# Opening of a fused attention and FFN kernel: v projected ahead of the scores, copies by one engine, more PSUM tiles, and the last output tile in two halves

## The chip, the core and the metric

One core of a Trainium2 chip. The metric is the time of one execution in microseconds (us), the median of several runs. A trace gives the span, from the first to the last instruction, which is some 1.8 us shorter than that time. All runs told here are of the fast state (granted TensorE clock 0.996 to 1.000 as a mean over the span). Within it, some executions, of either kernel, have a mean clock of 0.996 or 0.997; they take 0.5 to 2.3 us, mostly 1.5 to 2, longer than the other executions of the same kernel beside them (a clock halved for 3.4 us would be 0.997 over 520 us, and 1.7 us: an estimate from the run with late weights below). The ratios include them. Where it matters I also give the median of the executions with a clock of 0.998 or more, a cut that was made after the results were seen.

## The reference

Attention with keys and values projected along the sequence (from 1024 rows to 64), then a feed-forward layer with the quick Gelu on the joined heads:

```python
k_proj = np.einsum('ks,bhsd->bhkd', E, k)          # E, F: 64 x 1024; batch 8, heads 8, seq 1024, head dim 64
v_proj = np.einsum('ks,bhsd->bhkd', F, v)
scores = scale * np.matmul(q, k_proj.transpose(0, 1, 3, 2))
attn = softmax(scores)                             # cut: max, exp, sum
out = np.matmul(attn, v_proj)
x = out.transpose(0, 2, 1, 3).reshape(8192, 512)
h = x @ w_in                                       # 512 x 2048
g = h * (1.0 / (1.0 + np.exp(-1.702 * h)))
return g @ w_out                                   # 2048 x 512
```

## The kernel before

The FFN runs in 16 blocks of 512 tokens. In a block, 16 groups ("slots" 0 to 15) of four 128x512 matmuls make the hidden layer (FFN1), and 64 matmuls make the output (FFN2, eight more slots of eight). The attention of later blocks is put in between, at the slots named by `at(block, slot, ...)`. The order of every engine is fixed by the program. The program's PSUM tiles come from three pools: four general tiles (`ps_f`), two for token products (`ps_d`) and two for transposes (`ps_n`); a tile that comes round again must wait until its last reader is done.

The opening, before block 0 can start: heads are handled in pairs, `tok` multiplies exp(scores) with v and divides, `x_tr` transposes the result into `xT`, which FFN1 reads.

```python
    def v_out(b, v_ps, p0, n):                      # copies projected v out of PSUM
        for i in range(n):
            p = p0 + i
            for r, t in ((LO, p % 2), (HI, 1 - p % 2)):
                if b < 2:
                    cp = nc.scalar.copy if b == 0 and t == p % 2 else nc.vector.tensor_copy
                    cp(vxs[b][r, 2 * p + t, :D], v_ps[HI, 2 * i + t, :])
        # ... (the branch for b > 0)

    # tok(h, p, half): d_ps = ps_d.tile(...); 2 matmuls; rd = 1 / d_ps[..., D:]; x_sb = d_ps[..., :D] * rd   (VectorE)
    # x_tr(h, p, half): n_ps = ps_n.tile(...); 2 transposes; nc.vector.tensor_copy(xT ..., n_ps)

    # in ffn1, after the four matmuls into h_ps:
        if j > 0 or ts.start > 0 or fc > 4:
            nc.scalar.activation(gts[j][:, fc, ts], h_ps, AF.Gelu_apprx_sigmoid)
        else:                                       # tanh lives in the table of exp: no table switch yet
            t_sb = work.tile([P, n], F32, name="t_sb", bufs=3)
            nc.scalar.activation(t_sb, h_ps, AF.Tanh, scale=0.851)
            nc.vector.tensor_scalar(t_sb, t_sb, 0.5, 0.5, op0=ALU.mult, op1=ALU.add)
            nc.vector.tensor_tensor(gts[j][:, fc, ts], t_sb, h_ps, op=ALU.mult)

    # the opening, in TensorE's order
    for g in range(2):
        k_half(proj0(0, 4 * g, 4), g)               # k of heads 0-3, 4-7
        warm(3)                                     # fillers: matmuls on zeros
    q_tr(0, 0)()
    warm(3)
    for u in range(2):
        scores(0, u, 0)()
    v_out(0, proj0(1, 0, 4), 0, 2)                  # v of heads 0-3
    warm(2)
    tok(0, 0, 0)()
    tok(0, 1, 0)()
    # ... v of heads 4-5, x_tr, tok, v of heads 6-7, x_tr, tok, q_tr(0, 1), x_tr

    order = [(half, fc) for fcs in (range(12), range(12, FC)) for half in range(2) for fc in fcs]   # block 0
    at(0, 4, gelu_table)                            # switch ScalarE's table after slot 4
    # ... block 2:
        at(2, O + u, scores(4, u))
        at(2, O + 3 + u, scores(5, u))
    at(2, O + 5, norm(4, 0))
```

Block 0 is done in halves of 256 tokens: first slots 0 to 11 of the first half, so it can start with the attention of half the tokens. The order of the loads: E and F, k (two pieces), q (first quarter), v (three pieces), q (second quarter), input weights `w_in` in slices 0 to 5 of 256 columns, q (second half), slices 6 and 7, then `w_out`. Slice i serves slots 2i and 2i+1. They are issued by GpSimd, and every one waits until the load eight places ahead of it has landed.

```python
    for i in range(6):
        load_w_in(i)
    load_kv(q, qt, 0, "q0_sb", H, JB, JB)
    for i in range(6, 8):
        load_w_in(i)
```

The softmax here doesn't subtract the row's maximum and nothing guards it: scores larger than these inputs give would overflow.

Of the kernel before, what the change touches and what calls it, by code (L numbers as in the profile page):

```python
# [9 lines left out]
F32 = mybir.dt.float32  # L10
BF16 = mybir.dt.bfloat16
AF = mybir.ActivationFunctionType
ALU = mybir.AluOpType
# [4 lines left out]
def kernel(ctx, tc, q, k, v, E, F,  # L18
                                                     moe_w_in, moe_w_out, out):
    nc = tc.nc  # L20
    B, H, S, D = q.shape
    KP, _ = E.shape
    DM, DFF = moe_w_in.shape
    P = 128
# [92 lines left out]
    def f_tile(shape, dt=F32):  # L117
        return ps_f.tile(shape, dt, name="f_ps")

    def warm(n):  # L120
        w_ps = f_tile([P, TB])
        for _ in range(n):
            nc.tensor.matmul(w_ps, zeros[:, :P], zeros, start=True, stop=True)  # L123
# [25 lines left out]
    def proj0(e, h0, n):  # L149
        ps = f_tile([P, n, D])  # L150
        for j in range(J):
            nc.tensor.matmul(ps, eft[:, j, :], (kt, vt)[e][0][:, h0:h0 + n, j, :],  # L152
                             start=(j == 0), stop=(j == J - 1))
        return ps
# [11 lines left out]
                                ident[:KP, :KP])  # L166
        nc.vector.tensor_copy(kts[b % 2][:, p0:p0 + n, :], t_ps)

    def v_out(b, v_ps, p0, n):
        for i in range(n):  # L170
            p = p0 + i
            for r, t in ((LO, p % 2), (HI, 1 - p % 2)):
                if b < 2:
                    cp = nc.scalar.copy if b == 0 and t == p % 2 else nc.vector.tensor_copy
                    cp(vxs[b][r, 2 * p + t, :D], v_ps[HI, 2 * i + t, :])
        if b > 0:
            vv = v_ps[HI].rearrange("k (u x) d -> k u x d", x=4)
            for r, xs_ in ((LO, X_LO), (HI, X_HI)):
                nc.vector.tensor_copy(vqs[b % 2][r].rearrange("k (u e) d -> k u e d", e=2), vv[:, :, xs_, :])
# [44 lines left out]
    def scores(h, u, half=None):  # L224
        b, c = divmod(h, NB2)
        j0, n = (c * JB, JB) if half is None else (c * JB + half * JB // 2, JB // 2)
        ts = slice(j0 * P - c * TB, (j0 + n) * P - c * TB)

        def go():
            if h not in expT:  # L230
                expT[h] = att.tile([P, HP, TB], BF16, name="expT", bufs=3)
            s_ps = [f_tile([P, n * P]) for _ in range(2)]
            four(s_ps, [kts[b % 2][:, 2 * u + i, :] for i in range(2)],
                 [qT[b][:, j0:j0 + n, 2 * u + i, :] for i in range(2)])
            for i in range(2):
                nc.scalar.activation(expT[h][:, 2 * u + i, ts], s_ps[i], AF.Exp, scale=scale)  # L236
        return go
# [4 lines left out]
    def x_of(h):  # L242
        if h not in xT:
            xT[h] = att.tile([P, KC, TB], BF16, name="xT", bufs=3)
        return xT[h]
# [17 lines left out]

    def tok(h, p, half):
        def go():
            d_ps = ps_d.tile([P, 4, D + 1], F32, name="d_ps")
            for i in range(2):
                t = 2 * half + i
                nc.tensor.matmul(d_ps[:, 2 * i:2 * i + 2, :].rearrange("s t d -> s (t d)"),  # L269
                                 expT[h][:, p, t * P:(t + 1) * P],  # L270
                                 vxs[h // NB2][:, 2 * p:2 * p + 2].rearrange("r t d -> r (t d)"),
                                 start=True, stop=True)
            rd = work.tile([P, 4, 1], F32, name="rd")
            nc.vector.reciprocal(rd, d_ps[:, :, D:])  # L274
            xs[h, p, half] = work.tile([P, 4, D], BF16, name="x_sb", bufs=4)
            nc.vector.tensor_tensor(xs[h, p, half], d_ps[:, :, :D], rd.to_broadcast([P, 4, D]), op=ALU.mult)  # L276
        return go

    def x_tr(h, p, half):
        def go():  # L280
            x_sb = xs.pop((h, p, half)).rearrange("s (i t) d -> s i (t d)", i=2)
            n_ps = ps_n.tile([P, 2, P], BF16, name="n_ps")
            for i in range(2):
                nc.tensor.transpose(n_ps[:, i, :], x_sb[:, i, :], ident)  # L284
            nc.vector.tensor_copy(x_of(h)[:, p, half * TB // 2:(half + 1) * TB // 2],
                                  n_ps.rearrange("r i s -> r (i s)"))
        return go


# [2 lines left out]
    def ffn1(j, fc, ts=slice(0, TB)):  # L292
        if j not in gts:
            gts[j] = work.tile([P, FC, TB], BF16, name="gT")
        n = ts.stop - ts.start
        h_ps = f_tile([P, n])
        for kc in range(KC):
            nc.tensor.matmul(h_ps, w_in_sb[:, kc, fc * P:(fc + 1) * P], xT[j][:, kc, ts],  # L298
                             start=(kc == 0), stop=(kc == KC - 1))
        if j > 0 or ts.start > 0 or fc > 4:  # L300
            nc.scalar.activation(gts[j][:, fc, ts], h_ps, AF.Gelu_apprx_sigmoid)  # L301
        else:

            t_sb = work.tile([P, n], F32, name="t_sb", bufs=3)
            nc.scalar.activation(t_sb, h_ps, AF.Tanh, scale=0.851)
            nc.vector.tensor_scalar(t_sb, t_sb, 0.5, 0.5, op0=ALU.mult, op1=ALU.add)
            nc.vector.tensor_tensor(gts[j][:, fc, ts], t_sb, h_ps, op=ALU.mult)  # L307

    def ffn2(j, n, fcs):
        b, c = divmod(j, NB2)  # L310
        if j not in osb:
            osb[j] = work.tile([P, JB, DM], F32, name="o_sb")
        if fcs.start == 0:
            o_ps[n] = f_tile([P, DM])
        for fc in fcs:
            nc.tensor.matmul(o_ps[n], gts[j][:, fc, n * P:(n + 1) * P], w_out_sb[:, fc, :],  # L316
                             start=(fc == 0), stop=(fc == FC - 1))
        if fcs.stop == FC:
            nc.scalar.copy(osb[j][:, n, :], o_ps.pop(n))  # L319
            ov = out[b * S:(b + 1) * S, :].rearrange("(p j) m -> p j m", j=J)  # L320
            if j == NBLK - 1:
                nc.sync.dma_start(out=ov[:, c * JB + n, :], in_=osb[j][:, n, :])
            elif n == JB - 1:
                nc.sync.dma_start(out=ov[:, c * JB:(c + 1) * JB, :], in_=osb[j])
# [3 lines left out]
    def at(j, slot, *fs):  # L328
        fill.setdefault((j, slot), []).extend(fs)
# [4 lines left out]
        k_half(proj0(0, 4 * g, 4), g)  # L334
        warm(3)
    q_tr(0, 0)()
    warm(3)
    for u in range(2):
        scores(0, u, 0)()
    v_out(0, proj0(1, 0, 4), 0, 2)  # L340
    warm(2)
    tok(0, 0, 0)()
    tok(0, 1, 0)()
    v_out(0, proj0(1, 4, 2), 2, 1)
    x_tr(0, 0, 0)()
    x_tr(0, 1, 0)()
    tok(0, 2, 0)()
    v_out(0, proj0(1, 6, 2), 3, 1)
    x_tr(0, 2, 0)()
    tok(0, 3, 0)()  # L350
    q_tr(0, 1)()
    x_tr(0, 3, 0)()
# [6 lines left out]
        at(0, 8 + p, x_tr(0, p, 1))  # L359
    at(0, 20, q_tr(0, 2))  # L360
    at(0, 23, q_tr(0, 3))
    at(0, 4, gelu_table)
    for u in range(2):
        at(0, Q + u, scores(1, u))
    at(0, Q + 1, gelu_table)
# [8 lines left out]
    for u in range(2):  # L374
        at(1, O + u, scores(2, u))
        at(1, O + 3 + u, scores(3, u))
        at(2, O + u, scores(4, u))
        at(2, O + 3 + u, scores(5, u))
    for p in range(HP):
        at(1, O + 2 + p, tok(2, p, 0), tok(2, p, 1))  # L380
        at(1, O + 3 + p, x_tr(2, p, 0), x_tr(2, p, 1))
# [67 lines left out]
```

## Time and profile before

| | |
|---|---|
| time, median | 520.63 us (3 runs, 520.62 to 521.99) |
| time, median of all six runs beside the changed kernel | 521.38 us |
| span of the profiled run (time 521.62 us) | 519.8 us |
| TensorE busy | 97% |
| chain that ended last | TensorE 95%, VectorE 2%, DMA 1%, ScalarE 1% |

How to read the lines: PE is TensorE's matmuls, PEld its weight loads, DVE VectorE, ACT ScalarE, POOL GpSimd (here it only issues loads). "L316" is a line of the kernel. In lists in order of time the columns are start, duration, engine, line, operation, output<-inputs, and in brackets the idle time of that engine just before and what ended it. TensorE is a pipeline: a matmul of 512 columns shows 0.38 us but the next one starts 0.216 us later.

Which line is what, in the kernel before: L123 fillers, L152 projection, L175 copies of v, L202 transposes of q, L208 their copy, L222 scores and norm, L236 exp, L269 token products, L274 and L276 reciprocal and product, L284 transposes of x, L285 copies to xT, L298 FFN1, L301 Gelu, L305 tanh, L306 and L307 the rest of the sigmoid, L316 FFN2, L319 copy of the output, L322 its store. In the changed kernel most of them lie 3 lines later (L225, L239, L272, L287, L301, L304, L333), xT copies are L289, tanh L308, sigmoid L310 and L311.

What TensorE waited for, longest in total first (us in total, times, longest), in the profiled execution:

```profile
PE f_ps L132 <- ACT ef_sb L127: 1.6, 1, 1.6
...
PE n_ps L284 <- DVE x_sb L276: 0.8, 3, 0.4
PE d_ps L269 <- DVE x_sb L276: 0.6, 1, 0.6
PE f_ps L152 <- ACT expT L236: 0.4, 1, 0.4
```

The first of these is the wait for the constants E and F, at the very start. In order of time, block 2 and the end:

```profile
114.15 1.09 ACT L236 ACTIVATE expT<-f_ps 128x512 bf16<-128x512 f32 x2
...
114.54 0.66 PE L222 MATMUL f_ps<-qT,kt 64*64 64x512 bf16 x4
...
515.85 0.58 ACT L319 COPY o_sb<-f_ps 128x512 f32<-128x512 f32 x1 [2.87 <-PE f_ps L316]
```

The four score matmuls at 114.54 spread over 0.66 us where such four show 0.41 elsewhere: the second pair waits until an exp has freed its tile. After the last output copy (ends 516.43) it takes 3.37 us until the span ends.

### The profile page before, as it was taken

How to read it: one execution, taken by the hardware profiler on the slowest of the kernel's cores; microseconds unless marked ns; L12 is line 12 of the kernel's file. 1: busy time of each engine (PE TensorE's matmuls, PEld its weight loads, DVE VectorE, ACT ScalarE, POOL GpSimd, SP SyncE). 2: the span in 40 equal slices, each digit the busy share in tenths (PEclk: the TensorE clock that was granted, in tenths of full speed). 3: DMA queues.
4: the chain of work that ended last, by engine and by line, in shares of the span. 5: the costliest groups of instructions: out<-in, count | busy, mean ns of one | idle time of the engine just before them, and what ended most of it. 6: DMA issues, size and time to landing. Idle time of an engine off the chain costs nothing.

```text
span 519.8 us, 6658 instructions
## 1 busy us (share of the span) xinstructions
PE 506.2 (97%) x2792; PEld 232.5 (45%) x2843; DVE 253.8 (49%) x242; ACT 263.3 (51%) x437; POOL 77.3 (15%) x96
## 2 busy tenths in 40 slices
PE   7899999999999999999999999999999999999996
PEld 3575454443444444444444444444444444444442
DVE  2552344674865480827648183664808265560000
ACT  1376355464546547364555645465473646344351
POOL 6442620821510015000420000000000000000000
PEclk9999999999999999999999999999999999999999
DMA  9999999999996019760594302060200101010102
GB/s 168 197 203 206 218 183 166 169 184 157 230 162 161 1 81 155 94 163 0 123 173 124 72 10 77 1 162 0 82 5 1 81 1 81 1 81 1 81 1 81
DMA packets 113806, 53.78 MB, mean 103 GB/s; under 512 B 87664, under 2 KB 111216, under 8 KB 111856
## 3 DMA queue, kind: packets, MB, share of 16 engines
q0 software_dynamic: 84384, 29.37, 50.2%
q1 hardware_dynamic: 29312, 23.73, 16.3%
q8 instruction: 22, 0.36, 0.3%
q10 hardware_dynamic: 80, 0.26, 0.2%
q14 instruction: 8, 0.07, 0.0%
HBM read 59.24 MB, written 16.78 MB: 146 GB/s over the span
## 4 chain that ended last, share of the span: by engine, by line
PE 95%; DVE 2%; DMA 1%; ACT 1%; issue 1%; ACTq 0%
PE f_ps L316 43%; PE f_ps L298 42%; PE f_ps L144 2%; PE f_ps L222 2%; PE d_ps L222 1%; PE n_ps L222 1%; DMA ef_f<-in_E_dram 1%; PE f_ps L152 1%; PE f_ps L123 1%; PE n_ps L284 1%; PE d_ps L269 0%; DVE x_sb L276 0%; PE f_ps L205 0%; PE f_ps L202 0%; DVE gT L307 0%
## 5 line engine op out<-in xcount | busy, mean ns | idle before, releaser
L256 DVE RECIPROCAL rden<-d_ps 128x512 f32<-128x512 f32 x52 | 174.3, 3353 | 149.7 <-PE d_ps L222 149.7
L316 PE MATMUL f_ps<-w_out_sb,gT 128*128 128x512 bf16 x996 | 228.6, 379 | 1.8 <-issue 0.3
L298 PE MATMUL f_ps<-xT,w_in_sb 128*128 128x512 bf16 (+1 forms) x1066 | 226.6, 366 | 1.6 <-DVE gT L307 0.2
L301 ACT ACTIVATE gT<-f_ps 128x512 bf16<-128x512 f32 (+1 forms) x267 | 153.4, 575 | 85.7 <-PE f_ps L298 84.8
L298 PEld LDWEIGHTS <-w_in_sb 128*128 128x128 bf16 x1088 | 104.8, 98 | 116.1 <-issue 4.8
L316 PEld LDWEIGHTS <-gT 128*128 128x128 bf16 x1024 | 97.3, 98 | 122.3 <-issue 11.3
L319 ACT COPY o_sb<-f_ps 128x512 f32<-128x512 f32 x64 | 37.5, 586 | 137.0 <-PE f_ps L316 123.4
L63 POOL DMA_DIRECT2D q_sb<-in_q_dram x56 | 49.1, 896 | 67.2 <-DMA k_sb<-in_k_dram 27.1
L236 ACT ACTIVATE expT<-f_ps 128x512 bf16<-128x512 f32 (+1 forms) x68 | 35.3, 576 | 13.5 <-PE f_ps L222 13.4
L257 DVE TENSOR_TENSOR xT<-n_ps,rden 128x512 bf16<-128x512 f32 x52 | 36.0, 692 | 5.4
L57 POOL DMA_DIRECT2D k_sb<-in_k_dram x9 | 7.8, 864 | 107.6 <-PE f_ps L144 105.6
L236 ACT ACT_TABLE_LOAD x13 | 16.7, 1283 | 4.7 <-PE f_ps L222 4.5
L240 ACT ACT_TABLE_LOAD x14 | 18.0, 1283 | 0.2
L222 PE MATMUL f_ps<-qT,kt 64*64 64x512 bf16 (+1 forms) x136 | 13.8, 386 | 0.0
L144 PE MATMUL f_ps<-k_sb,eft 128*64 128x512 bf16 x56 | 13.4, 382 | 0.0
L144 PE MATMUL f_ps<-v_sb,eft 128*64 128x512 bf16 x56 | 13.4, 382 | 0.0
L274 DVE RECIPROCAL rd<-d_ps 128x4 f32<-128x4 f32 x24 | 4.2, 175 | 15.5 <-PE d_ps L269 15.4
L208 DVE COPY qT<-f_ps 128x1024 bf16<-128x1024 bf16 x8 | 5.5, 692 | 11.7 <-PE f_ps L202 6.8
L276 DVE TENSOR_TENSOR x_sb<-d_ps,rd 128x256 bf16<-128x256 f32 x24 | 10.2, 425 | 0.8
L222 PEld LDWEIGHTS <-kt 64*64 64x64 bf16 x136 | 4.1, 103 | 14.2 <-issue 14.2
L123 PE MATMUL f_ps<-zeros 128*128 128x512 bf16 x26 | 9.1, 493 | 1.2 <-DVE zeros L105 1.2
L222 PE MATMUL d_ps<-expT,ones 64*64 64x512 bf16 x104 | 10.2, 382 | 0.0
(48 smaller groups left out, 115.2 us busy)
## 6 DMA issues: line engine op xcount, KB each, us to landing
out_dram<-o_sb SPq DMA_DIRECT2D x15, 1024.0 KB, 4.2
k_sb<-in_k_dram POOLq DMA_DIRECT2D x7, 1024.0 KB, 12.9
v_sb<-in_v_dram POOLq DMA_DIRECT2D x7, 1024.0 KB, 10.7
q_sb<-in_q_dram POOLq DMA_DIRECT2D x56, 128.0 KB, 11.1
w_in_sb<-in_moe_w_in_dram POOLq DMA_DIRECT2D x8, 256.0 KB, 12.5
w_out_sb<-in_moe_w_out_dram POOLq DMA_DIRECT2D x4, 512.0 KB, 14.7
k_sb<-in_k_dram POOLq DMA_DIRECT2D x2, 512.0 KB, 7.7
out_dram<-o_sb SPq DMA_DIRECT2D x4, 256.0 KB, 2.0
```

What stands on the lines that cost most here:

```text
L63: nc.gpsimd.dma_start(out=qt[b][:, j], in_=qv[:, j])
L123: nc.tensor.matmul(w_ps, zeros[:, :P], zeros, start=True, stop=True)
L144: nc.tensor.matmul(kvps[b][r], eft[:, j, e * KP:(e + 1) * KP], (kt, vt)[e][b][:, :, j, :], start=(j == 0), stop=(j == J - 1))
L222: nc.tensor.matmul(outs[i][r], lhsTs[i][ri], rhss[i][ri], start=True, stop=True)
L236: nc.scalar.activation(expT[h][:, 2 * u + i, ts], s_ps[i], AF.Exp, scale=scale)
L240: nc.scalar.preload_act_table(AF.Gelu_apprx_sigmoid)
L256: nc.vector.reciprocal(rden, d_ps[i])
L257: nc.vector.tensor_tensor(x_of(h)[:, 2 * u + i, :], n_ps[i], rden, op=ALU.mult)
L298: nc.tensor.matmul(h_ps, w_in_sb[:, kc, fc * P:(fc + 1) * P], xT[j][:, kc, ts], start=(kc == 0), stop=(kc == KC - 1))
L301: nc.scalar.activation(gts[j][:, fc, ts], h_ps, AF.Gelu_apprx_sigmoid)
L316: nc.tensor.matmul(o_ps[n], gts[j][:, fc, n * P:(n + 1) * P], w_out_sb[:, fc, :], start=(fc == 0), stop=(fc == FC - 1))
L319: nc.scalar.copy(osb[j][:, n, :], o_ps.pop(n))
```

## The change

Its intent: fill TensorE's holes in the opening, by getting v out of PSUM before it is needed, by taking work off VectorE's chain there, and by letting token products use the general pool; clear the stall in block 2; and shorten the way from the last matmul to the end. The whole diff:

```diff
--- before.py
+++ after.py
@@ -166,13 +166,16 @@
                                 ident[:KP, :KP])
         nc.vector.tensor_copy(kts[b % 2][:, p0:p0 + n, :], t_ps)
 
-    def v_out(b, v_ps, p0, n):
-        for i in range(n):
-            p = p0 + i
-            for r, t in ((LO, p % 2), (HI, 1 - p % 2)):
-                if b < 2:
-                    cp = nc.scalar.copy if b == 0 and t == p % 2 else nc.vector.tensor_copy
-                    cp(vxs[b][r, 2 * p + t, :D], v_ps[HI, 2 * i + t, :])
+    def v_out(b, v_ps, p0, n, cp=nc.vector.tensor_copy):
+        if b < 2:
+            if n == 1:
+                for r, t in ((LO, p0 % 2), (HI, 1 - p0 % 2)):
+                    cp(vxs[b][r, 2 * p0 + t, :D], v_ps[HI, t, :])
+            else:
+                vv = v_ps[HI].rearrange("k (u x) d -> k u x d", x=4)
+                vx = vxs[b][:, 2 * p0:2 * (p0 + n), :D].rearrange("k (u x) d -> k u x d", x=4)
+                for r, xs_ in ((LO, X_LO), (HI, X_HI)):
+                    cp(vx[r, :, xs_], vv[:, :, xs_])
         if b > 0:
             vv = v_ps[HI].rearrange("k (u x) d -> k u x d", x=4)
             for r, xs_ in ((LO, X_LO), (HI, X_HI)):
@@ -263,7 +266,7 @@
 
     def tok(h, p, half):
         def go():
-            d_ps = ps_d.tile([P, 4, D + 1], F32, name="d_ps")
+            d_ps = f_tile([P, 4, D + 1]) if (h, half) == (0, 0) and p > 1 else                 ps_d.tile([P, 4, D + 1], F32, name="d_ps")
             for i in range(2):
                 t = 2 * half + i
                 nc.tensor.matmul(d_ps[:, 2 * i:2 * i + 2, :].rearrange("s t d -> s (t d)"),
@@ -282,8 +285,8 @@
             n_ps = ps_n.tile([P, 2, P], BF16, name="n_ps")
             for i in range(2):
                 nc.tensor.transpose(n_ps[:, i, :], x_sb[:, i, :], ident)
-            nc.vector.tensor_copy(x_of(h)[:, p, half * TB // 2:(half + 1) * TB // 2],
-                                  n_ps.rearrange("r i s -> r (i s)"))
+            cp = nc.scalar.copy if (h, half) == (0, 0) else nc.vector.tensor_copy
+            cp(x_of(h)[:, p, half * TB // 2:(half + 1) * TB // 2], n_ps.rearrange("r i s -> r (i s)"))
         return go
 
 
@@ -297,19 +300,33 @@
         for kc in range(KC):
             nc.tensor.matmul(h_ps, w_in_sb[:, kc, fc * P:(fc + 1) * P], xT[j][:, kc, ts],
                              start=(kc == 0), stop=(kc == KC - 1))
-        if j > 0 or ts.start > 0 or fc > 4:
+        if j > 0 or ts.start > 0 or fc > 3:
             nc.scalar.activation(gts[j][:, fc, ts], h_ps, AF.Gelu_apprx_sigmoid)
         else:
 
             t_sb = work.tile([P, n], F32, name="t_sb", bufs=3)
             nc.scalar.activation(t_sb, h_ps, AF.Tanh, scale=0.851)
-            nc.vector.tensor_scalar(t_sb, t_sb, 0.5, 0.5, op0=ALU.mult, op1=ALU.add)
-            nc.vector.tensor_tensor(gts[j][:, fc, ts], t_sb, h_ps, op=ALU.mult)
+            g = gts[j][:, fc, ts]
+            nc.vector.scalar_tensor_tensor(g, t_sb, 1.0, h_ps, op0=ALU.add, op1=ALU.mult)
+            nc.vector.tensor_scalar_mul(g, g, 0.5)
 
     def ffn2(j, n, fcs):
         b, c = divmod(j, NB2)
+        ov = out[b * S:(b + 1) * S, :].rearrange("(p j) m -> p j m", j=J)
         if j not in osb:
             osb[j] = work.tile([P, JB, DM], F32, name="o_sb")
+        if j == NBLK - 1 and n == JB - 1:
+
+            if fcs.start == 0:
+                for i, cp in enumerate((nc.scalar.copy, nc.vector.tensor_copy)):
+                    ms = slice(i * DM // 2, (i + 1) * DM // 2)
+                    l_ps = f_tile([P, DM // 2])
+                    for fc in range(FC):
+                        nc.tensor.matmul(l_ps, gts[j][:, fc, n * P:(n + 1) * P], w_out_sb[:, fc, ms],
+                                         start=(fc == 0), stop=(fc == FC - 1))
+                    cp(osb[j][:, n, ms], l_ps)
+                    nc.sync.dma_start(out=ov[:, c * JB + n, ms], in_=osb[j][:, n, ms])
+            return
         if fcs.start == 0:
             o_ps[n] = f_tile([P, DM])
         for fc in fcs:
@@ -317,7 +334,6 @@
                              start=(fc == 0), stop=(fc == FC - 1))
         if fcs.stop == FC:
             nc.scalar.copy(osb[j][:, n, :], o_ps.pop(n))
-            ov = out[b * S:(b + 1) * S, :].rearrange("(p j) m -> p j m", j=J)
             if j == NBLK - 1:
                 nc.sync.dma_start(out=ov[:, c * JB + n, :], in_=osb[j][:, n, :])
             elif n == JB - 1:
@@ -334,19 +350,16 @@
         k_half(proj0(0, 4 * g, 4), g)
         warm(3)
     q_tr(0, 0)()
-    warm(3)
+    warm(2)
+    v_out(0, proj0(1, 0, 4), 0, 2)
     for u in range(2):
         scores(0, u, 0)()
-    v_out(0, proj0(1, 0, 4), 0, 2)
-    warm(2)
-    tok(0, 0, 0)()
-    tok(0, 1, 0)()
     v_out(0, proj0(1, 4, 2), 2, 1)
-    x_tr(0, 0, 0)()
-    x_tr(0, 1, 0)()
-    tok(0, 2, 0)()
-    v_out(0, proj0(1, 6, 2), 3, 1)
-    x_tr(0, 2, 0)()
+    for p in range(3):
+        tok(0, p, 0)()
+    v_out(0, proj0(1, 6, 2), 3, 1, nc.scalar.copy)
+    for p in range(3):
+        x_tr(0, p, 0)()
     tok(0, 3, 0)()
     q_tr(0, 1)()
     x_tr(0, 3, 0)()
@@ -359,7 +372,7 @@
         at(0, 8 + p, x_tr(0, p, 1))
     at(0, 20, q_tr(0, 2))
     at(0, 23, q_tr(0, 3))
-    at(0, 4, gelu_table)
+    at(0, 3, gelu_table)
     for u in range(2):
         at(0, Q + u, scores(1, u))
     at(0, Q + 1, gelu_table)
@@ -374,8 +387,8 @@
     for u in range(2):
         at(1, O + u, scores(2, u))
         at(1, O + 3 + u, scores(3, u))
-        at(2, O + u, scores(4, u))
-        at(2, O + 3 + u, scores(5, u))
+        at(2, O + 2 * u, scores(4, u))
+        at(2, O + 3 + 2 * u, scores(5, u))
     for p in range(HP):
         at(1, O + 2 + p, tok(2, p, 0), tok(2, p, 1))
         at(1, O + 3 + p, x_tr(2, p, 0), x_tr(2, p, 1))
```

The new sigmoid rests on 0.5·(t+1)·h = (0.5·t+0.5)·h.

## The prediction

> **What bounds the kernel now.** I read the page first (busy shares, slices, chain), then the same per stretch, then TensorE's waits, then the order of time where TensorE is not full. The busy shares and the chain:
>
> ```profile
> PE 506.2 (97%) x2792; PEld 232.5 (45%) x2843; DVE 253.8 (49%) x242; ACT 263.3 (51%) x437; POOL 77.3 (15%) x96
> ...
> PE 95%; DVE 2%; DMA 1%; ACT 1%; issue 1%; ACTq 0%
> ```
>
> TensorE is the bound almost everywhere; other engines hold about 4% of the chain. The busy time by stretch (window, its length, busy us of each engine) shows where:
>
> ```profile
> 15.00:20.00 5.00, 3.98 (x37) 2.38 (x36) 2.46 (x8) 1.84 (x7) 3.02 (x4) 1.00 1.49 193
> 20.00:25.00 5.00, 4.12 (x50) 2.48 (x49) 3.94 (x14) 1.66 (x7) 2.22 (x3) 1.00 1.45 197
> 25.00:30.00 5.00, 4.23 (x41) 3.50 (x41) 4.31 (x16) 3.99 (x10) 2.37 (x3) 1.00 1.45 197
> 30.00:35.00 5.00, 4.95 (x49) 4.32 (x48) 1.47 (x6) 3.69 (x11) 2.62 (x3) 1.00 1.30 204
> ```
>
> From 15 to 30 us TensorE idles 1.02 + 0.88 + 0.77 = 2.67 us, and some of what it does there is filler on zeros; from 30 us on it is full. From 160 to 500 us it is busy 338.1 of 340. So a change of order in the opening has at most some 3 us to win, and nothing can reach 2% (10.4 us). The chain of waits, in order of time, inside that stretch:
>
> ```profile
> 16.51 1.05 PE f_ps L152 x8
> 17.56 0.02 issue
> 17.58 0.22 ACT vx L175
> 17.80 0.02 issue
> 17.82 0.24 DVE vx L175
> 18.06 0.02 issue
> 18.09 0.22 ACT vx L175
> 18.31 0.02 issue
> 18.33 0.23 DVE vx L175
> 18.56 0.03 issue
> 18.59 0.20 DVE rd L274
> ```
>
> The v projection starts only after the scores and their first exp, and its four copies follow one another, alternating between two engines: 17.58 to 18.56, about 1 us. Then come reciprocal, product, transpose, copy, and at last the first FFN group, whose fourth matmul waits; two more waits follow (order of time: start, us, engine, line):
>
> ```profile
> 23.25 0.27 PE L298 MATMUL f_ps<-xT,w_in_sb 128*128 128x256 bf16 x1 [0.20 <-DVE xT L285]
> ...
> 27.00 1.28 ACT L240 ACT_TABLE_LOAD   x1
> ...
> 28.93 0.29 PE L269 MATMUL d_ps<-vx,expT 128*128 128x130 bf16 x2 [0.62 <-DVE x_sb L276]
> ```
>
> The reader is to see three milestones: last xT piece used at 23.25, table loaded at 28.28, TensorE held to 28.93 by a VectorE still finishing five sigmoid pieces.
>
> **What the Trainium skill says.** PSUM — Partial Sum Buffer, section PSUM bank collisions raise a hardware error: two different engines on one bank and quadrant collide, so such accesses must be ordered by semaphores. The trace agrees: the ACT and DVE copies above never overlap although their destinations differ, so two engines there bring no parallelism. VectorE: DVE Perf Modes, section What auto-detection actually checks: the four-per-cycle mode needs 16-bit operands and SBUF on both sides. In the trace PSUM copies cost 0.230 us for 64x64 and 0.417 for 64x256, about 1 ns an element plus 0.17; the fast bf16 multiply is in no run yet. ScalarE: Activation LUTs, section What ACT_TABLE_LOAD costs: about 1283 ns for the load; the trace has 1.28, and the next activation starts 0.01 us after it. TensorE: Matmul & The Clock Gate, section What's actually happening: the clock falls after an idle window of about 3.4 us. The longest TensorE wait here is 1.6 us and the granted clock is 1.00 in every row above.
>
> **The change, part by part.**
>
> 1. *v of heads 0 to 3 before the scores, three filler matmuls gone.* In the compiled order TensorE now does q transposes, 2 fillers, v projection, scores. Fillers start at 14.89 and cost 0.216 us each to issue, so the projection starts at 15.33 (v landed about 14.86: the DMA queue's own wait for it ends at 14.90). With its 1.03 us it ends at 16.36, not 17.54. Its copies become two of 64x128 on VectorE: 0.17 + 128 ns = 0.30 each, 16.40 to 17.00. Scores then issue from 16.22; exps at about 16.56, 16.84, 17.12. The fourth score tile must wait for a bank until about 17.0 (a new wait of some 0.35 us), so the v of heads 4 and 5 runs 17.15 to 17.76.
> 2. *Token products and transposes.* Heads 0 and 1 are multiplied at 17.62 instead of 18.10. VectorE finishes the copies for heads 4 and 5 at 18.27, then a reciprocal and a product take 0.55 us per piece (18.81 to 19.36 in the trace): products end at 18.94, 19.49, 20.04. The third and fourth token tiles use the general PSUM pool, so they wait for no release of the two-buffer pool. v of heads 6 and 7 ends at 19.03, is copied on ScalarE by 19.5; the fourth token piece runs at 20.2, its product ends at 21.15.
> 3. *xT copies on ScalarE.* Four copies of 0.287 leave VectorE; on ScalarE a 128x256 pass takes about 0.38 and follows its like after 0.28. The fourth starts at 21.5 and ends about 21.9. VectorE makes the second qT (0.69) meanwhile, ending at 21.84. The first FFN group completes from 21.9 instead of 23.25: **1.35 us gained**.
> 4. *Sigmoid pieces.* Before: 5 pieces of 0.376 + 0.421 = 0.80 on VectorE. After: 4 pieces of about 0.42 (product from PSUM) plus an estimated 0.15 (bf16 in SBUF) = 0.57, and the PSUM tile is free after the first instead of the second. VectorE has 5 x 0.80 - 4 x 0.57 = 1.7 us less before it turns to the token pieces of the second half. The table load comes one piece earlier: last tanh ends near 24.95, table 26.24 (28.28 before), first Gelu pass out at 26.65, and the group of slot 8 starts at about 26.7 against 29.06. So 2.35 in all by this sum. I chose not to believe all of it: every wait was chained by hand with no slack, so I keep 0.85 of the further 1.0: **2.2 us for the opening**. Check on size: idle 2.67 plus three fillers 0.65 is 3.3, of which 2.2 is two thirds.
> 5. *Block 2: the second pair of scores a slot later.* Before, ScalarE loads the exp table at 112.85, exps follow from 114.15, the next scores wait for their tiles: 114.54 to 115.28 for four matmuls that take 0.34 elsewhere. **0.4 us gained**; the other moved pair sits with the norm in slot 5 and waits for nothing I can see.
> 6. *Last output tile in halves.* 32 matmuls of 256 columns issue every 0.115 (36 in 4.31 us at 31.37, less one latency of 0.27, by 35) = 3.69, against 16 x 0.216 = 3.45: 0.24 lost. The last latency is 0.27, not 0.38: 0.11 won. The last copy is 256 wide on VectorE, about 0.42 instead of 0.58: 0.16 won. The transfer is 128 KB; 256 KB took 2.0 us to land, so I estimate 0.2 won. **Net 0.2 gained**.
> 7. The eight 64x64 copies of batch 1 become two of 64x256 (1.92 to about 0.87 on VectorE); TensorE did not wait there: 0.
>
> Sum 2.2 + 0.4 + 0.2 = 2.8; I take **2.6**, because stretches that come earlier meet transfers that do not. 520.6 - 2.6 = **518.0 us**.
>
> **Rivals.**
> - *Transfers become the bound.* Weights are loaded on a fixed schedule that TensorE does not drive; the DMA queue waits show input-weight slices landing about 22.9, 23.7, 25.0, 26.3, 27.65, and output-weight quarters up to 43.2. My new times need them at 23.5, 24.4, 25.4, 26.7, 28.0 and 44.6: margins of 0.3 to 1.4 us. If landings slip, the opening gains 1.3 only: 519.0.
> - *ScalarE becomes the bound.* It takes on four copies of 0.38. For it: the last xT waits on ScalarE. Against: 1.84 us busy of 5 in 15:20, 1.66 in 20:25. Worst case it adds one copy: 518.4.
> - *PSUM tiles.* Scores after v take the banks of v; the wait I put at 0.35 could be 0.8, and the third and fourth token tiles use up two more general tiles. 518.5.
> - *Clock.* Fewer fillers, but no idle stretch I foresee exceeds 1 us, so the clock stays: 0. If it halved for one window of 3.4 us, +1.7 us.
> - *All of it works and more*: if the whole 2.67 of idle plus fillers went, 517.0.
>
> **Range and chances.** The two low fast runs of before agree to 0.01 us, the third is 1.4 higher, so noise belongs in the range: 516.9 (everything works) to 519.5 (transfers bind and half of the small gains fail). Faster by 2% would need 510.2, four times the idle that is touched; slower by 2% a broken steady state, whose order is unchanged. 0.01, 0.98, 0.01.
>
> **What would show it.** Right: v projection ends near 16.4 and its two copies touch; the fourth FFN matmul near 21.9; the Gelu table done near 26.2; slot 8 near 26.7 to 27; four matmuls at block 2's second scores within 0.35 and no break near 115; last matmul to end of span about 3.5 us instead of 4.0; TensorE busy share up by about half a point. Wrong: DMA named as what ended a TensorE wait before 45 us; a clock below 1.00 before 30 us; waits on ScalarE's xT copies over 0.5; matmuls of the last tile apart by more than 0.12; or gains in the opening that vanish again by 60 us.

## The result, and the profile after

The changed kernel took 518.25 us (median of 6 runs, 517.9 to 519.12), the kernel before 521.38 us (6 runs, 520.62 to 521.99). The ratio is 0.9945, 95% interval 0.9932 to 0.9957. A ratio here is the mean time of one kernel's fast runs over that of the other's of the same rounds, so it is not quite the ratio of the medians quoted. 0.0055 of 521 us is 2.9 us; 2.6 us and 518.0 us had been foretold. Run again in a later session, it took 518.18 against 520.72 us, ratio 0.9948 (0.9932 to 0.9964).

The profiled span is 516.5 us instead of 519.8. The chain of the changed kernel, and its busy time by stretch:

```profile
PE 94%; DMA 4%; POOL 1%; issue 0%; DVE 0%; DVEq 0%; POOLq 0%
```

```profile
15.00:20.00 5.00, 3.68 (x44) 2.49 (x45) 2.68 (x10) 2.21 (x8) 3.12 (x4) 1.00 1.48 194
20.00:25.00 5.00, 4.70 (x54) 3.18 (x53) 3.23 (x10) 3.66 (x12) 2.12 (x3) 1.00 1.45 197
25.00:30.00 5.00, 4.88 (x49) 3.90 (x47) 3.67 (x15) 3.81 (x10) 2.47 (x4) 1.00 1.45 197
30.00:35.00 5.00, 5.00 (x58) 4.26 (x57) 0.69 (x1) 3.80 (x11) 2.63 (x3) 1.00 1.32 204
```

Between 20 and 30 us TensorE's idle time fell from 1.65 to 0.42 us. (From 15 to 20 us it rose, from 1.02 to 1.32, with three fillers fewer in the opening.) VectorE and ScalarE have left the chain, and DMA has come in, from 1% to 4%. Where it comes in (weight loads of TensorE in order of time):

```profile
24.12 0.77 PEld L301 LDWEIGHTS <-w_in_sb 128*128 128x128 bf16 x8 [0.16 <-DMA w_in_sb<-in_moe_w_in_dram]
...
25.26 0.33 PEld L301 LDWEIGHTS <-w_in_sb 128*128 128x128 bf16 x4 [0.15 <-DMA w_in_sb<-in_moe_w_in_dram]
...
26.60 0.33 PEld L301 LDWEIGHTS <-w_in_sb 128*128 128x128 bf16 x4 [0.24 <-DMA w_in_sb<-in_moe_w_in_dram]
```

Slots 4, 6 and 8 of the first half now start when their weight slice lands. In the chain in order of time, the opening is two loads, one after the other, and nothing else; the first was in flight from 4.31 us on, the second could be issued when it had landed, and its own landing let slot 8 go (by a margin of 0.24 us only):

```profile
4.31 10.60 DMA v_sb<-in_v_dram
14.91 0.28 issue
15.19 11.37 DMA w_in_sb<-in_moe_w_in_dram
26.56 0.05 issue
26.61 0.61 PE f_ps L301 x4
```

Block 2 and the end, in order of time:

```profile
111.83 1.08 ACT L239 ACTIVATE expT<-f_ps 128x512 bf16<-128x512 f32 x2
...
113.94 0.41 PE L225 MATMUL f_ps<-qT,kt 64*64 64x512 bf16 x4
...
513.01 0.42 DVE L327 COPY o_sb<-f_ps 128x256 f32<-128x256 f32 x1 [50.91 <-PE f_ps L325]
```

The four score matmuls stand at 0.41, and after the last copy (ends 513.43) 3.07 us remain.

Milestones, in us from the start of the span:

| | before | changed | gained so far |
|---|---|---|---|
| q transposes of the opening start | 14.32 | 13.60 | 0.7 |
| slot 8 of the first half starts | 29.06 | 26.61 | 2.45 |
| first of block 2's moved scores | 112.36 | 110.05 | 2.31 |
| first FFN1 matmul of block 3 | 127.20 | 124.26 | 2.94 |
| first FFN2 matmul of the last block | 501.84 | 498.90 | 2.94 |
| end of the span | 519.8 | 516.5 | 3.3 |

So 2.3 come from the opening, 0.6 from block 2, nothing from 370 us of unchanged order, and 0.4 from the end. But the first row is a warning: the programs are the same up to there, and one trace is 0.7 us ahead. Their first lines tell why:

```profile
6.01 1.28 ACT L127 ACT_TABLE_LOAD   x1 [6.01 <-DMA ef_f<-in_E_dram]
```

and, for the changed kernel,

```profile
5.31 1.28 ACT L127 ACT_TABLE_LOAD   x1 [5.31 <-DMA ef_f<-in_E_dram]
```

The constants landed 0.7 us later in the one profiled execution of the kernel before. How much of the 2.3 is such luck is a question for the experiments. The share of time that TensorE is busy rose from 97.4 to 98.1%, and from the last matmul's end to the end of the span it is 3.6 us instead of 4.0, both about as foretold.

### The profile page after: what moved, and what is told of

Its sections match the earlier page's. It is cut to its first block, busy times and chain, and to the rows that moved or that the text cites. A ratio compares the mean times of both kernels' runs of the same rounds, so it can differ in the third digit from the quotient of the medians.

```text
span 516.5 us, 6729 instructions
## 1 busy us (share of the span) xinstructions
PE 506.9 (98%) x2856; PEld 233.2 (45%) x2856; DVE 251.4 (49%) x231; ACT 264.0 (51%) x439; POOL 77.4 (15%) x96
## 4 chain that ended last, share of the span: by engine, by line
PE 94%; DMA 4%; POOL 1%; issue 0%; DVE 0%; DVEq 0%; POOLq 0%
PE f_ps L333 43%; PE f_ps L301 42%; PE f_ps L144 3%; DMA w_in_sb<-in_moe_w_in_dram 2%; DMA v_sb<-in_v_dram 2%; PE f_ps L225 2%; PE d_ps L225 1%; PE n_ps L225 1%; PE f_ps L325 1%; PE n_ps L287 0%; PE d_ps L272 0%; PE f_ps L208 0%; POOL k_sb L57 0%; PE f_ps L205 0%; POOL q_sb L57 0%
## 5 line engine op out<-in xcount | busy, mean ns | idle before, releaser
L333 PEld LDWEIGHTS <-gT 128*128 128x128 bf16 x1008 | 95.7, 98 | 120.4 <-issue 11.1
L225 PE MATMUL n_ps<-expT,vq 64*64 64x512 bf16 x104 | 10.0, 376 | 0.0
```

The lines of the kernel that those rows point to most:

```text
L225: nc.tensor.matmul(outs[i][r], lhsTs[i][ri], rhss[i][ri], start=True, stop=True)
L333: nc.tensor.matmul(o_ps[n], gts[j][:, fc, n * P:(n + 1) * P], w_out_sb[:, fc, :], start=(fc == 0), stop=(fc == FC - 1))
```

## The experiments

My theory, the sum: the opening, block 2 and the tail add up, and in the opening each part (v first, one-engine copies, xT on ScalarE, the sigmoid) is worth what it takes off the chain of engines. The rival: transfers cap the opening. Then the parts of the opening do not add up, taking one back costs little, and pushing a load back costs dear.

### Each of the three parts alone

**Opening alone.** The change without these two edits:

```diff
-        at(2, O + 2 * u, scores(4, u))
-        at(2, O + 3 + 2 * u, scores(5, u))
+        at(2, O + u, scores(4, u))
+        at(2, O + 3 + u, scores(5, u))
     ... (and the branch `if j == NBLK - 1 and n == JB - 1` in ffn2 taken out)
```

> The kernel before with the opening of the change alone (slot move and halved last tile left out). Theory of the sum: the opening carries 2.2 to 2.3 us of the gain, so the ratio to before is about 0.9957; the group of slot 8 starts near 26.6 us, as in the changed kernel. Rival (the gain lies mostly in the slot move and the tail): ratio above 0.998.

Measured: 519.02 us against 520.56, ratio 0.997 (0.9958 to 0.9982), so 1.6 us with an interval of 0.9 to 2.2. Slot 8 started at 26.37, as the theory had it; the ratio lies between what the theory and the rival had said. In this trace TensorE waits for no weight slice, so here the engines set slot 8: in the changed kernel engines and slices are within 0.25 us of each other.

**Block 2 alone.** The kernel before with only

```diff
-        at(2, O + u, scores(4, u))
-        at(2, O + 3 + u, scores(5, u))
+        at(2, O + 2 * u, scores(4, u))
+        at(2, O + 3 + 2 * u, scores(5, u))
```

> The kernel before with the second pair of block 2's scores moved a slot later, nothing else. Theory: 0.4 us foretold, 0.6 read off the two traces (the way from the first of these scores to the next block's first matmul 14.84 us before, 14.21 after), ratio about 0.999. Rival: those waits are given back at the norm that now shares the slot: 0.0 us and the way stays at 14.8.

Measured: 519.87 us against 520.56, ratio 0.9991 (0.9979 to 1.0003). The trace is sharper: from the first of these scores (113.16) to block 3 (127.38) it is 14.22 us, against 14.83 in three traces that keep the old slots (14.84 in the kernel before, 14.83 in the tail alone and in the run with late weights below). 0.61 us, of which the stall explains 0.40 (0.74 us from the four matmuls to the next where 0.34 is usual). For the rest, the moved scores now stand directly in front of the norm, and there is one break less between FFN matmuls and four-matmul groups: such a group takes 0.34 us before FFN matmuls but 0.24 before another of its kind. That is 0.1. The last 0.1 lies in the FFN matmuls: with a break less, two runs of eight (1.83 us each) have become one of sixteen (3.55).

**Tail alone.** The kernel before with only the branch for the last tile in ffn2.

```diff
+        if j == NBLK - 1 and n == JB - 1:
+            if fcs.start == 0:
+                for i, cp in enumerate((nc.scalar.copy, nc.vector.tensor_copy)):
     ... (as in the change)
```

> The kernel before with the last output tile in halves, nothing else. Theory: 0.2 us foretold, 0.36 read off the two traces (from the last block's first output matmul to the end 17.96 us before, 17.60 after), ratio about 0.9994. Rival: weight loads of the 32 half-wide matmuls cost more than the shorter copy and transfer give: 17.96 or more.

Measured: 520.26 against 520.56 us, ratio 0.9996 (0.9984 to 1.0009), not to be told from nothing by its time. In its trace the last block's FFN2 and end take 17.56 us (500.64 to 518.2); with whole tiles 17.96 (before), 17.98 (block 2 alone) and 17.95 (opening alone). So 0.4 us is real: the copy 0.42 instead of 0.58, the way from its end to the end of the span 3.04 instead of 3.37, and TensorE loses 0.04 only (14.02 instead of 13.98 from the first matmul to the last's end).

The three ratios alone multiply to 0.9957, 2.2 us, against 0.9945 and 0.9948 for the whole. With these intervals that agrees. But the opening alone is 1.6 us by time, and the two traces had said 2.3. The tail's trace gives the reason: with the kernel before's opening, but constants landed by 4.62 us, slot 8 starts at 27.85 and not at 29.06. Over all traces (ACT's first table load shows when the constants of E landed):

| opening of | constants of E | q transposes start | slot 8 |
|---|---|---|---|
| before, profiled for the prediction | 6.01 | 14.32 | 29.06 |
| before, in the tail's run | 4.62 | 13.52 | 27.85 |
| before, in block 2's run (k landed late) | 4.60 | 15.53 | 29.85 |
| changed | 5.31 | 13.60 | 26.61 |
| changed, again | 5.00 | 13.31 | 26.50 |
| changed, opening alone | 4.72 | 13.45 | 26.37 |

The old opening hangs on a chain of engines from the constants and k, and moves with their landing: 2 us between the best and the worst of these three. In the worst, late k also brought a lower clock (0.66 from 10 to 15 us), so landing alone is not all of it. Nor is it all for the trace behind the prediction: from q transposes to slot 8 it takes 14.74 us, against 14.33 and 14.32 in the other two. The 0.4 are two of VectorE's sigmoid instructions, usually 0.28 to 0.30 us, that here took 0.61 and 0.41 and ended 0.09 us after GpSimd (POOL) had issued a load (at 24.49 and 27.12):

```profile
22.97 1.52 POOL L95 DMA_DIRECT2D w_out_sb<-in_moe_w_out_dram  x2 [1.98 <-DMA w_in_sb<-in_moe_w_in_dram]
23.97 0.61 DVE L306 TENSOR_SCALAR t_sb<-t_sb 128x256 f32<-128x256 f32 x1 [0.78 <-ACT t_sb L305]
...
26.38 0.74 POOL L95 DMA_DIRECT2D w_out_sb<-in_moe_w_out_dram  x1 [0.59 <-DMA w_in_sb<-in_moe_w_in_dram]
26.80 0.41 DVE L306 TENSOR_SCALAR t_sb<-t_sb 128x256 f32<-128x256 f32 x1
```

So of the 1.21 us between this trace and the tail's, 0.80 were there when the q transposes started, and some 0.4 came from these two.

The new one sat at 26.4 to 26.6 in all three of its traces. Against the best old one the opening gained 1.2 to 1.5 us, against the one I predicted from 2.5.

### Is the opening now held by transfers?

**A load pushed back, in the changed kernel.** Weight slices 4 and 5 trade places with the second half of q:

```diff
-    for i in range(6):
+    for i in range(4):
         load_w_in(i)
     load_kv(q, qt, 0, "q0_sb", H, JB, JB)
-    for i in range(6, 8):
+    for i in range(4, 8):
         load_w_in(i)
```

> The changed kernel with the last two of the six early slices of the input weights loaded behind the third piece of q instead of ahead of it (some 2.6 us later, by the landings in the trace). Theory that transfers are now what bounds the opening: the group of slot 8 starts when its slice lands, about 29.1 instead of 26.6 us, and nearly all of it is lost, ratio about 0.9985. Rival (engines bound it, transfers have slack of their own): 0.9945 as the changed kernel, or at most 0.5 us of the 2.6 lost.

Measured: 522.05 us against 520.56, ratio 1.002 (1.0008 to 1.0032): not 2.6 but 3.9 us lost, more than the whole change had won. Slot 8, in order of time, and then the stretches (clock in the third last column):

```profile
29.14 0.61 PE L301 MATMUL f_ps<-xT,w_in_sb 128*128 128x256 bf16 x4 [2.70 <-DMA w_in_sb<-in_moe_w_in_dram]
```

```profile
25.00:30.00 5.00, 2.30 (x26) 1.80 (x24) 2.16 (x10) 2.40 (x6) 2.14 (x4) 1.00 1.45 196
28.00:30.00 2.00, 0.86 (x10) 0.81 (x11) 0.10 (x1) 0.21 (x1) 1.36 (x2) 1.00 1.45 196
30.00:32.00 2.00, 2.00 (x15) 1.49 (x14) 1.19 (x5) 0.94 (x3) 1.13 (x2) 0.67 1.41 200
32.00:34.00 2.00, 2.00 (x13) 1.44 (x12) 0.29 (x1) 0.77 (x2) 1.50 (x2) 0.50 1.25 209
34.00:36.00 2.00, 2.00 (x19) 1.81 (x18) 0.00 (x0) 1.49 (x4) 0.25 (x1) 0.98 1.24 205
```

The first part is as the transfer theory says: slot 8 at 29.14 instead of 26.61, 2.5 us. The rest is the clock: TensorE waited 2.70 us, and from 30 to 34 us its clock is granted at 0.67 and 0.50. What is not granted there adds up to 2 x 0.33 + 2 x 0.50 + 2 x 0.02 = 1.7 us of full speed. (By single microseconds it is 0.84, 0.50, 0.50, 0.50, 0.96 from 30 to 35 us: half for some 3.4 us, from about 1.5 us after the wait was over.) 2.5 + 1.7 = 4.2; the FFN2 of block 0 indeed starts 4.0 us later, at 43.36 instead of 39.35. The six executions say the same: two kept a clock of 1.000 and took 520.43 and 520.71 us, 2.3 to 2.5 more than the changed kernel's 518.18; the other four, the traced one among them, had 0.997 and took 521.92 to 522.35.

**The same edit in the kernel before.**

> The kernel before with the same two weight slices loaded behind the third piece of q. In the kernel before the group of slot 8 started at 27.9 to 29.1 us while its slice landed near 26.3, so there are 1.5 to 2.8 us of slack against a slice that comes some 2.6 us later. Theory (transfers bind only after the change): at most 1.3 us lost, ratio 1.000 to 1.0025, and no halved clock, against 3.9 us lost by the same edit in the changed kernel. Rival (the edit is dear by itself, wherever it is made): about 3.9 us lost, 1.0075.

Measured: 521.9 against 520.85 us, ratio 1.0018 (1.0005 to 1.0031), 0.9 us lost. Slot 8:

```profile
29.02 0.61 PE L298 MATMUL f_ps<-xT,w_in_sb 128*128 128x256 bf16 x4 [0.91 <-DMA w_in_sb<-in_moe_w_in_dram]
```

It stands at 29.02 here too, where the slice lands, but without the edit it would have stood at 27.85: the kernel before had 1.2 to 1.3 us of slack against this load, the changed kernel has none. The clock stayed at 1.00 in the stretches from 25 to 35 us of the traced execution; two of the other four had a mean of 0.996, as had three of the eleven of the kernel before. Without these it is 521.76 against 520.74, 1.0 us.

### The parts of the opening

Four runs on one chip: the changed kernel, and three with one part taken back.

> The changed kernel itself once more, as the base for the three runs beside it on the same chip. Ratio 0.9945 as before, or up to 0.9957 (the product of the three parts run alone); slot 8 at its weight slice's landing, about 26.5 us, whether the constants of E land at 4.7 or at 6.0 us.

Measured: 518.18 against 520.72 us, 0.9948. Slot 8 at 26.50, after a wait of 0.23 us for its weight slice.

**v late again.** The old order and fillers, the rest of the change kept:

```diff
-    warm(2)
-    v_out(0, proj0(1, 0, 4), 0, 2)
+    warm(3)
     for u in range(2):
         scores(0, u, 0)()
+    v_out(0, proj0(1, 0, 4), 0, 2)
+    warm(2)
+    tok(0, 0, 0)()
+    tok(0, 1, 0)()
     ... (and on as before)
```

> The changed kernel with the v projection back behind the scores and the old order and fillers (copies still by one engine, xT copies on ScalarE, new sigmoid, more PSUM tiles kept). Theory of the sum (my prediction): the first FFN group completes near 23 us instead of 21.8 and the total loses about 1.0 us, ratio about 0.9963. Rival (the landing of the weight slices sets the time): the first group is late, but slot 8 still starts within 0.4 us of its place and the total loses at most 0.4 us.

Measured: 518.75 us, ratio 0.9962 (0.9944 to 0.9981).

**The old sigmoid** (five pieces, table after slot 4):

```diff
-        if j > 0 or ts.start > 0 or fc > 3:
+        if j > 0 or ts.start > 0 or fc > 4:
     ...
-            g = gts[j][:, fc, ts]
-            nc.vector.scalar_tensor_tensor(g, t_sb, 1.0, h_ps, op0=ALU.add, op1=ALU.mult)
-            nc.vector.tensor_scalar_mul(g, g, 0.5)
+            nc.vector.tensor_scalar(t_sb, t_sb, 0.5, 0.5, op0=ALU.mult, op1=ALU.add)
+            nc.vector.tensor_tensor(gts[j][:, fc, ts], t_sb, h_ps, op=ALU.mult)
     ...
-    at(0, 3, gelu_table)
+    at(0, 4, gelu_table)
```

> The changed kernel with the five sigmoid pieces and the later table load of before. Theory of the sum: the table is in 0.8 us later and the whole loses 0.8 to 1.0 us, ratio about 0.996, with TensorE waiting on VectorE or ScalarE near 27 us. Rival (weight slices set the time): slot 8 waits for whichever is later, so at most 0.4 us lost.

Measured: 518.99 us, ratio 0.9969 (0.995 to 0.9988).

**xT copies on VectorE:**

```diff
-            cp = nc.scalar.copy if (h, half) == (0, 0) else nc.vector.tensor_copy
+            cp = nc.vector.tensor_copy
```

> The changed kernel with the first four xT copies back on VectorE. Theory of the sum: VectorE's chain of products gets 3 copies of 0.29 us in it, the first FFN group completes 0.5 to 0.9 us later and the total loses about as much, ratio about 0.9957. Rival (weight slices): the first group is late but slot 8 is where it was, total within 0.2 us of the changed kernel.

Measured: 518.16 us, ratio 0.9953 (0.9935 to 0.9972).

**Two engines for the copies of v**, as in the kernel before, in the new order (a session later):

```diff
-    def v_out(b, v_ps, p0, n, cp=nc.vector.tensor_copy):
-        ... (the new branch for b < 2)
+    def v_out(b, v_ps, p0, n, _cp=None):
+        for i in range(n):
+            ...
+                    cp = nc.scalar.copy if b == 0 and t == p % 2 else nc.vector.tensor_copy
```

> The changed kernel with the copies of v again cut in 64x64 pieces that alternate between two engines. Theory (two engines on one PSUM bank take turns): the four copies of heads 0 to 3 take about 1.0 us instead of 0.60 and never overlap; the first FFN group 0.2 to 0.5 us later; the total within 0.3 us of the changed kernel (ratio 0.9945 to 0.9953) because the weight slice still sets slot 8. Rival (two engines do run side by side): copies done in about 0.5 us.

Measured: 518.67 against 520.85 us, ratio 0.9964 (0.9948 to 0.9979).

The ratios differ by less than their intervals. Without the executions of 0.996 and 0.997 the medians are 518.17 with nothing taken back, 518.15 (xT copies), 518.67 (v first), 518.88 (new sigmoid), and 518.59 against 520.74 in the later session (two engines, where the whole change had won 2.4); that is 0, 0.5, 0.7 and some 0.25 us, about the 1.5 of the opening alone in sum. What each part is worth is read from slot 8, in traces whose q transposes all start between 13.15 and 13.91:

| taken back | last xT piece used in slot 0 | slot 8 starts | held there by | ratio |
|---|---|---|---|---|
| nothing | | 26.50 to 26.61 | weight slice, 0.23 to 0.24 | 0.9945, 0.9948 |
| xT copies on ScalarE | 21.91 | 26.63 | VectorE's product, 0.15 | 0.9953 |
| v first | | 26.78 | engines: no wait for a slice | 0.9962 |
| new sigmoid | | 27.10 | VectorE's product, 0.5 | 0.9969 |
| one engine for v's copies | | 27.17 | engines: no wait for a slice | 0.9964 |

So the rival is right about slot 8 for two parts: without the xT copies on ScalarE, or without v first, it is only 0.1 and 0.2 to 0.3 us later. Its reason holds in part. Beside the changed kernel on the same chip, the first tanh is 0.40 and 0.62 us later (22.22 and 22.44 against 21.82), so 0.3 us went into the waits for weight slices, which these two traces no longer have. The rest of the 0.5 to 0.9 and 1.2 us that I expected was never there: the engines lost less. The rival is wrong for the other two parts, where the engines are clearly later than the slice. The last one I had put at 0.3 us; the copies did take turns as I expected, 0.98 us from 16.16 to 17.14 where one engine takes 0.60, but I had missed what comes behind them:

```profile
16.16 0.21 ACT L175 CAST vx<-f_ps 64x64 bf16<-64x64 f32 x1 [8.63 <-PE f_ps L152]
16.40 0.23 DVE L175 CAST vx<-f_ps 64x64 bf16<-64x64 f32 x1 [1.11 <-ACT vx L175]
16.66 0.21 ACT L175 CAST vx<-f_ps 64x64 bf16<-64x64 f32 x1 [0.30 <-DVE vx L175]
16.90 1.21 ACT L236 ACTIVATE expT<-f_ps 128x256 bf16<-128x256 f32 x4
16.91 0.23 DVE L175 CAST vx<-f_ps 64x64 bf16<-64x64 f32 x1 [0.28 <-ACT vx L175]
17.33 0.30 PE L222 MATMUL f_ps<-qT,kt 64*64 64x256 bf16 x2 [0.88 <-ACT expT L236]
```

With v in front of the scores, ScalarE's two copies of v stand ahead of the exps in its own order. Exps start at 16.90 although their scores were issued at 16.05, and the scores' last pair waits 0.88 us for the tile of the first exp; in the changed kernel exps start 0.34 us after the scores (16.27 after 15.93) and that wait is 0.37. So "copied by one engine" is not only two copies in place of four: with two engines, v in front (slot 8 at 27.17) did worse than v late with one engine (26.78). No run takes back the added PSUM tiles or the fillers alone.

### Two parts alone, on the kernel before

**v first alone** (new order, new copies and fillers; sigmoid, xT copies and PSUM pools as before):

> The kernel before with the v projection in front, its copies by one engine and the fewer fillers; sigmoid, xT copies and PSUM pools of before. Theory of the sum: about 1.0 us won alone (ratio 0.998), first FFN group near 21.9, slot 8 near 27. If the parts overlap through the weight slices, this one and the sigmoid alone add up to more than the opening alone won (0.997).

Measured: 520.32 against 520.85 us, ratio 0.9998 (0.998 to 1.0017). By the ratio that is nothing won, against 1.0 us expected. But two of its six executions had a clock of 0.996 or 0.997 (522.33 and 521.8 us); the other four have a median of 520.0, against 520.74 of the kernel before, 0.7 us. The trace, at clock 1.000, says the same: slot 8 is at 27.43, 0.4 us better than the best old opening, although its q transposes started 0.34 us later (13.86 against 13.52). Its largest wait in the opening:

```profile
18.84 0.27 PE L272 MATMUL d_ps<-vx,expT 128*128 128x130 bf16 x2 [1.10 <-DVE rd L277]
```

The third token product comes straight behind the first two and must wait 1.10 us for a tile of the two-tile pool, until VectorE has read the first (in the changed kernel, where it has a tile of the general pool, it waits 0.42, for the copy of v). So v first pays without more PSUM tiles too, and this wait is what they take away; what that is worth in time no run shows.

**The sigmoid alone:**

> The kernel before with the new sigmoid (four pieces, one product from PSUM and one fast multiply, table a piece earlier), nothing else. Theory of the sum: the table is in about 0.8 us earlier, slot 8 too, ratio about 0.9985. Rival: slot 8 keeps its place because VectorE is held by the xT copies and products, ratio 1.000.

Measured: 520.1 against 520.85 us, ratio 0.9984 (0.9969 to 0.9998), 0.8 us. Slot 8 at 27.07, against 27.85 with the same start (q transposes 13.50 and 13.52, last xT piece used at 22.43 and 22.45): 0.78 us, as foretold, though the table is in only 0.56 us earlier (26.62 against 27.18). Expected had been that, if weight slices made the parts overlap, this run and the one before would add up to more than the opening alone won. They do not show it: 0.2 and 1.6 per mille by the ratios, 0.7 and 0.65 us without the low clocks, against 3.0 per mille and 1.5 us.

No version that beats the changed kernel came out of this. In the stretch of slots 4 to 8 the slices land 1.1 to 1.3 us apart, each carrying 256 KB, and TensorE asks for them as fast; an earlier start would wait for the same landings. Fewer bytes ahead of slice 4 would be needed, and all that is loaded ahead of it is used before slot 8. This last step is argued, not tried.

## Why the prediction was right, point by point

**The total**: 518.0 foretold, 518.25 and 518.18 measured; 2.6 us foretold, 2.9 and 2.7 by the ratios. The steady state did not move, as said. It came out because two errors nearly cancel.

**Steps 1 to 4, the opening: mechanism right, size wrong.** "2.2 us for the opening" measured 1.6 alone by its time, and 1.2 to 1.5 by slot 8 against an old opening whose data came early. I had taken "29.06" for the place of slot 8 in the kernel before from one trace, whose constants landed at 6.01 us and whose time of 521.62 was a microsecond over its median, and then took the gain off the median, 520.63. That I took 0.15 off the sum of 2.35 as slack was a guess, and names no cause. The end of the step, "the group of slot 8 starts at about 26.7", was right: 26.61 and 26.50.

- Step 1: v projection foretold from 15.33 with its copies 16.40 to 17.00; measured 14.95, 16.04 to 16.64, 0.4 early. The q transposes were 0.7 early, but TensorE then stood some 0.35 us until v had landed (0.18 of it shown as idle). "A new wait of some 0.35 us" for the fourth score tile: 0.37. But its tile came free by the first exp and not by the copies of v.
- Step 2: products 0.55 us apart foretold; they start at 18.31, 18.86, 19.41. That the extra PSUM tiles matter was in the step as a remark; v first alone shows 1.10 us of waiting without them.
- Step 3: "completes from 21.9 instead of 23.25". The fourth matmul of slot 0 is not listed by itself in the changed kernel's trace; its tanh starts at 22.08, against 23.56. Of these 1.48 us 0.72 are the earlier start: from the q transposes to this tanh it takes 9.24 us in both the trace before and the tail's, and 8.48 to 8.58 in the changed opening's three. So "1.35 us gained" measures some 0.7. About 0.4 of what is missing is TensorE standing before the v projection (1.35 to 1.46 us from the q transposes to it, 1.01 in the sum); the rest I can't place.
- Step 4: "5 x 0.80 - 4 x 0.57 = 1.7 us less" on VectorE: the fast multiply takes 0.23, not the 0.15 that I estimated (less than the 0.17 that I had read off as the fixed part of a copy), so a piece is 0.65 and the saving 1.4. The table was in at 25.96 (24.68 + 1.28), foretold 26.24. The effect on slot 8 was 0.78 alone, where the sum had a further 1.0.

**Step 5, block 2**: 0.4 foretold, 0.61 by trace; the stall was 0.40; the break saved by standing next to the norm, 0.2, was not in the sum.

**Step 6, the tail**: 0.2 foretold, 0.4 by trace. The loss of TensorE was overrated (0.24 less 0.11 foretold, 0.04 measured: matmuls of half width came every (3.66 - 0.27) / 31 = 0.109 us instead of 0.115), and the smaller transfer gave 0.3 instead of 0.2.

**Step 7**: VectorE's shorter copies for batch 1 gave nothing, as said: first scores of block 2 are 2.31 us ahead, slot 8 was 2.45.

**Rivals.** "Transfers become the bound" came true in part and without cost to the total: "margins of 0.3 to 1.4 us" were in fact none at slots 4, 6 and 8, where the waits are 0.16, 0.15 and 0.24 us. The prediction had named just this ("DMA named as what ended a TensorE wait before 45 us") as a sign of being wrong; the total was right all the same. With it the opening's end is set by the landing of slice 4, and that is part of why undoing v first or the xT copies alone costs less than by the sum. "Clock": 1.7 us for one halved window was the estimate; it did not happen in the changed kernel's twelve executions, and when a load pushed back made it happen, the clock that was missing came to 1.7.

## What to carry to other kernels

Before a gain is summed from one trace of a stretch that begins with loads, look at when those loads landed in it, and compare the execution's own time with the median: here late constants (0.8 us at the q transposes) and two stretched sigmoid instructions (0.4) made the old opening look 1.2 us worse than in its best trace. A chain of engines that is shortened until a load sets its end has a floor; push one load back to find out, and watch the clock, because a TensorE that waits for it may pay again in granted clock (here 1.7 us in four of six executions). List the clock of every execution before calling a mean a miss. Parts of a change that look like trimmings (here one engine for the copies) can decide what the main move pays: test the main move without them.

## What the Trainium skill lacked or had wrong

- TensorE: Matmul & The Clock Gate, section HAM oscillation, gives "no PE-idle gaps" longer than about 3.4 us as the rule. Here less was enough: after a wait of 2.70 us (TensorE busy 2.30 of the 5 us around it) the clock was 0.67 and 0.50 in the next two stretches of 2 us. In the run of block 2 alone a single wait of 1.27 us for k, with TensorE busy 2.81 of 5 us, was followed by 0.66 in the next 5 us.
- ScalarE: Activation LUTs, section What ACT_TABLE_LOAD costs, counts a drain of about 1380 ns on top of the load for every switch. The load agrees (1.28 us); the drain does not show: in the changed kernel the last tanh ends at 24.66, the load starts at 24.68 and the first Gelu at 25.98, 1.30 us later.
- SBUF — State Buffer, section Who interferes with whom, says that VectorE's two-port modes and GpSimd block each other, but not for how long an issue of a load does so. Here the sigmoid's instruction with one tensor as input (128x256) took 0.23 us in 16-bit and 0.28 to 0.30 in 32-bit form. In the 14 traces 15 of them took longer: 0.28 to 0.53 us in 16-bit, 0.33 to 0.61 in 32-bit form. Each of these began at least 0.24 us after GpSimd had begun to issue a load, and ended 0.02 to 0.10 us after that issue did; others that began less than 0.18 us after the start of an issue were not stretched (0.29 us at 28.38 in the run of block 2 alone), where the page has the block last for the whole instruction. No run isolates it.
- None of the pages has the cost of a break between FFN matmuls and a group of four 64-row matmuls: 0.34 us for the group before FFN matmuls, 0.24 before another such group.
